# Three edits to the order of roundings in a fused attention and feed-forward kernel: ScalarE's rounding of g goes ahead of the next tanh, and the rounding of the softmax weights goes from ScalarE to VectorE

## The chip, the cores and the metric

The kernel runs on one core of one Trainium2 chip. The metric is the device time of one execution, in microseconds (us). Five queues matter: TensorE (PE in the profile; its weight loads are PEld), VectorE (DVE), ScalarE (ACT), GpSimd (POOL) and the DMA queue of SyncE (SP). Each works through its own instructions in order; an instruction waits at the head of its queue until what it reads is ready and what it writes is free.

## The reference

Four batches of 12480 rows, width 128, 49 agents. Attention goes through the agents, then a feed-forward layer of width 2048 with the activation h - tanh(h):

```python
a2k = softmax(scale * agents @ k^T)      # 49 x 12480 per batch
agent_v = a2k @ v                        # 49 x 128
q2a = softmax(scale * q @ agents^T)      # 12480 x 49
x = q2a @ agent_v                        # 12480 x 128
h = x @ w_in                             # 12480 x 2048
g = h - tanh(h)
out = g @ w_out                          # 12480 x 128
```

Everything is float32.

## The kernel before, in words

**Blocks, steps, pairs.** The rows are cut into 100 blocks of 500 (25 per batch). A block takes eight steps, each for two of the 16 chunks of the hidden width; so there are 800 steps. Two blocks are a pair of 16 steps, and `pos` (0 to 15) is the place of a step in its pair. The two matrices ahead of h are folded: `awh` and `awl` are the high and low part of `agent_v @ w_in` (98 rows: the 49 agents twice, for the high and low part of the weights), so that h comes from the softmax weights p in one product.

**One step.** For step k, in the names of the profile:

- `first_product` (`m1`, L537 and L538): four matmuls of 500 columns on TensorE make h(k) in PSUM, which has three buffers for h. It is issued two steps ahead.
- `tanhs` (`tanh`, L546): ScalarE makes y = tanh(c h). `squares` (`square`, L551): ScalarE makes z = y². Both are issued one step ahead.
- `product` (`mul`, L556): VectorE makes g = h z (for the small h of these inputs h - tanh(h) is a constant times that, to the accuracy needed). h comes from PSUM, z from SBUF.
- `high` (L589 on GpSimd, L587 on ScalarE): the high part gh of g, rounded to float32r, a format in which a matmul takes one pass. `low` (`low`, L594): VectorE makes gl = g - gh, one step later, behind the product of that step.
- `out` (`m2`, L606, L607, L609): six matmuls on TensorE, four that read gh and then two that read gl, are added in PSUM. It follows `low`, so TensorE's order is m1(k+2), m2(k-1), m1(k+3), m2(k).
- In every second block the last step (`PLAIN_PAIR`, pos 7 of a pair) is "plain": g isn't split at all; two chunks go through four-pass float32 matmuls (L603), and neither GpSimd's rounding nor VectorE's subtraction is made for it.

The rounding of g is GpSimd's in all steps but 39. Those 39 are the steps in which GpSimd has to subtract the row maximum of attention scores (`av`, L321): there `product` only leaves a mark (`ET.Activation`) in the list `r1`, and ScalarE makes gh one step later. They are at pos 1, 3 and 12 (`VS`) of those pairs in which the weighted sum over v of the next batch is made: 13 groups of keys for each of three batches.

**The side work.** For the next batch, `phase1` makes key scores (at pos 3, 5 and 14, `KS`, 13 pairs in all) and after that the sums over v (pos 1, 3, 12, another 13 pairs' worth). For the next pair of blocks, `q_softmax` makes the weights p from q: 64 small matmuls at pos 3, row maximum and copy at pos 4 with GpSimd's subtraction (L504), exp at pos 6, and at pos 8 the norm on VectorE: sum, add, reciprocal, multiply (L508 to L511). Its steps are parted by `yield`; `QGAPS` says how many steps lie between. At pos 9 ScalarE rounds p to its high part (L514), and at pos 10 GpSimd subtracts it from p (L516) for the low part. `q_transpose` (L524, L529) transposes both at pos 12 to 15. The first two of the 50 softmaxes are made before or early in the main loop with gaps of 1; 48 use `QGAPS`.

**What sets the order.** It is written out by hand: the loop in `fast` issues each step's parts in a fixed sequence, and `issue_order` chains the instructions of VectorE, ScalarE, GpSimd and TensorE in the order in which they were issued. In a step k the loop calls `tanhs(k + 1)`, then the copy of a finished block to its output (L770), then lets all side jobs advance by one `yield`, then `squares(k + 1)` (with the marked rounding of step k - 1 ahead of the square), `first_product(k + 2)`, `product(k)`, `low` for step k - 1, `out` for step k - 1.

Of the kernel before, what the change touches and what calls it, by code (L numbers as in the profile page):

```python
# [17 lines left out]
ET = mybir.EngineType  # L18
# [6 lines left out]
A = 49  # L25
# [6 lines left out]
TT = 126  # L32
# [31 lines left out]
AHEAD = 2  # L64
QL = 0
QS = 2
QGAPS = (1, 1, 0, 2, 2, 1, 1)
T0 = 12
T1 = 14
KS = (3, 5, 14)  # L70
# [4 lines left out]
def width(n):  # L75
    return min(BLK, N - n % NBLK * BLK)
# [22 lines left out]
class Build:  # L99
# [384 lines left out]
    def q_softmax(self, halves, qt, res, TT=TT, gaps=(1,) * 7):  # L484
        nc = self.nc
        yield from (None,) * gaps[0]
        ps = self.misc()
        for t in range(GT):
            b, at, w = halves[t // BT]
            at += min(t % BT * TT, w - TT)  # L490
            for r in range(0, TT, QUART):
                m = min(QUART, TT - r)
                to = ps[r : r + m, t * A : (t + 1) * A]
                nc.tensor.matmul(to, qt[:, at + r : at + r + m], self.ag[:, b, :], start=True, stop=True)  # L494
        yield from (None,) * gaps[1]
        pv = ps[:TT, : GT * A].rearrange("p (t a) -> p t a", a=A)
        m = self.small.tile([128, GT], F32, tag="qm", name="qm")
        e = self.small.tile([128, GT, A], F32, tag="qe", name="qe")
        ev = e[:TT]
        s = self.small.tile([128, GT], F32, tag="qs", name="qs")  # L500
        nc.vector.tensor_reduce(m[:TT], pv, axis=AX.X, op=ALU.max)
        nc.scalar.copy(ev, pv)  # L502
        yield from (None,) * gaps[2]
        nc.gpsimd.tensor_tensor(ev, ev, m[:TT, :, None].broadcast_to([TT, GT, A]), ALU.subtract)  # L504
        yield from (None,) * gaps[3]
        nc.scalar.activation(ev, ev, AF.Exp, scale=SCALE)
        yield from (None,) * gaps[4]
        nc.vector.tensor_reduce(s[:TT], ev, axis=AX.X, op=ALU.add)  # L508
        nc.vector.tensor_scalar(s[:TT], s[:TT], EPS, None, ALU.add)
        nc.vector.reciprocal(s[:TT], s[:TT])  # L510
        nc.vector.tensor_tensor(ev, ev, s[:TT, :, None].broadcast_to([TT, GT, A]), ALU.mult)  # L511
        yield from (None,) * gaps[5]
        pp = self.small.tile([128, GT, A2], F32R, tag="pp", name="pp")
        nc.scalar.copy(pp[:TT, :, :A], ev)  # L514
        yield from (None,) * gaps[6]
        nc.gpsimd.tensor_tensor(pp[:TT, :, A:], ev, pp[:TT, :, :A].bitcast(F32), ALU.subtract)  # L516
        res.append(pp)
# [132 lines left out]
    def fast(self):  # L650
        nc, tc = self.nc, self.tc
# [4 lines left out]
        qt, pp, pT = {}, {}, {}  # L656
# [5 lines left out]
        def q_job(p):  # L662
            pp[p] = []
            w = width(2 * p), width(2 * p + 1)
            halves = (blocks[2 * p][0], 0, w[0]), (blocks[2 * p + 1][0], w[0], w[1])
            return self.q_softmax(halves, qt.pop(p), pp[p], gaps=QGAPS if p > 1 else (1,) * 7)

# [4 lines left out]
        with ExitStack() as first:  # L672
# [34 lines left out]
            at = self.count() - 1  # L707
# [48 lines left out]
        r1, r2, done = [], [], []  # L756
# [21 lines left out]
                hs[k] = self.m1(self.aw[blocks[n][0]], pT[n][0], i, width(n))  # L778

        def tanhs(k):  # L780
            if k < len(steps):
                ys[k] = self.tanh(hs[k], width(steps[k][0]))

        def squares(k):
            for n, at in enumerate(r1):
                if at[3] is ET.Activation:
                    r1[n] = at[:3] + (self.high(at[2], True),)
            if k < len(steps):
                zs[k] = self.square(ys.pop(k))

# [22 lines left out]
        for k in range(AHEAD):  # L813
            first_product(k)
        tanhs(0)
        squares(0)
        for k, (n, i) in enumerate(steps):
            b = blocks[n][0]
            pos = (n % 2) * HP + i
            p = n // 2  # L820
            if n % NBLK == 0 and i == 0 and b + 1 < B:
                kq = self.phase1(b + 1)
            tanhs(k + 1)
            while done and done[0][1] < k - 1:
                finish(done.pop(0)[0])
# [9 lines left out]
            for gen in live:  # L835
                try:
# [3 lines left out]
                    pass  # L840
            live[:] = nxt
            squares(k + 1)
            first_product(k + AHEAD)
            begin = kq and n and pos in kq[0][0]
# [90 lines left out]
```

## Time and profile before

| what | value |
|---|---|
| median of 3 runs | 2160.22 us (2155.68 to 2160.96) |
| the profiled execution | 2158.05 us, span 2156.3 us |
| granted TensorE clock | 0.997 |
| VectorE busy | 1980.1 us of the span, 92% |
| ScalarE busy | 1814.4 us, 84% |
| GpSimd busy | 1387.0 us, 64% |
| rounding by ScalarE (L587) | 39 times, 1.037 us each |
| rounding of p by ScalarE (L514) | 50 times, 0.520 us each |

A row of the timeline is: start in us, duration in us, engine, line of the kernel, operation, tile written <- tiles read, shapes, count; in square brackets the idle time of the engine just before it and what ended it. A row of the waits is: engine and line that waited <- engine and line that released it: us in total, times, longest. A row of the windows is: stretch in us, its length, and the busy time and instructions of each engine. Matmul rows overlap, because matmuls are pipelined: the distance from start to start is what a matmul costs.

### The profile page before, as it was taken

What the parts mean: (1) busy time and instruction counts of PE and PEld (TensorE: products, weight loads), DVE (VectorE), ACT (ScalarE), POOL (GpSimd) and SP (SyncE); (2) the same over time, 40 slices, a digit from 0 to 9 for tenths busy, and PEclk for the clock granted to TensorE, in tenths of its full rate; (3) what the DMA queues carried; (4) which work ended last, traced back from release to release, by engine and by line L of the source; (5) the groups of instructions that cost most, each with busy time, mean ns of one, the idle gap of its engine ahead of it and who ended that gap; (6) DMA issues with size and microseconds to landing.
All of it is one profiled execution on the core that took longest, in us unless ns stands there. A gap on an engine that the chain in (4) does not pass through costs nothing.

```text
span 2156.3 us, 37634 instructions
## 1 busy us (share of the span) xinstructions
PE 2093.9 (97%) x14885; PEld 1633.4 (76%) x14885; DVE 1980.1 (92%) x2028; ACT 1814.4 (84%) x2136; POOL 1387.0 (64%) x857
## 2 busy tenths in 40 slices
PE   7999999999999999999999999999999999999998
PEld 7577777777777777777777777777777787877876
DVE  7899998889999998888999999888899999999998
ACT  3888888888888888888888888888888888988887
POOL 0466765556767665565676667656576777767776
PEclk9999999999999999999999999999999999999999
DMA  9222112110111121112002210121010010000000
GB/s 355 71 79 69 42 41 67 59 51 29 39 50 49 57 64 49 49 45 74 20 20 63 74 33 20 50 67 41 19 39 20 20 39 20 28 31 20 29 11 21
DMA packets 65352, 109.16 MB, mean 51 GB/s; under 512 B 3984, under 2 KB 44176, under 8 KB 65168
## 3 DMA queue, kind: packets, MB, share of 16 engines
q1 hardware_dynamic: 65168, 106.68, 15.1%
q8 instruction: 119, 1.95, 0.4%
q14 instruction: 65, 0.53, 0.1%
HBM read 81.10 MB, written 25.56 MB: 49 GB/s over the span
## 4 chain that ended last, share of the span: by engine, by line
PE 58%; DVE 22%; ACT 8%; issue 7%; POOL 4%; DMA 0%; POOLq 0%; SPq 0%; DVEq 0%; ACTq 0%
PE h L537 12%; PE misc L609 11%; DVE gl L594 11%; PE h L538 11%; PE misc L606 8%; PE misc L607 8%; DVE g L556 8%; POOL gh L589 3%; ACT z L551 2%; PE misc L336 2%; ACT gh L587 2%; PE misc L603 1%; ACT y L546 1%; PE misc L494 1%; PE h L249 1%
## 5 line engine op out<-in xcount | busy, mean ns | idle before, releaser
L589 POOL TENSOR_SCALAR gh<-g 128x1000 fp32r<-128x1000 f32 (+1 forms) x704 | 1214.0, 1724 | 600.2 <-DVE g L556 513.5
L546 ACT ACTIVATE y<-h 128x1000 f32<-128x1000 f32 (+1 forms) x800 | 805.9, 1007 | 270.5 <-PE h L538 267.0
L556 DVE TENSOR_TENSOR g<-h,z 128x1000 f32<-128x1000 f32 (+1 forms) x800 | 950.2, 1190 | 80.0 <-ACT z L551 74.4
L594 DVE TENSOR_TENSOR gl<-g,gh 128x1000 fp32r<-128x1000 f32 (+1 forms) x743 | 926.0, 1246 | 63.7 <-ACT gh L587 56.8
L551 ACT ACTIVATE z<-y 128x1000 f32<-128x1000 f32 (+1 forms) x800 | 834.4, 1043 | 14.5 <-DVE g L556 1.0
L537 PE MATMUL h<-pT,awh 98*128 98x500 f32 (+1 forms) x1600 | 669.8, 419 | 2.2 <-ACT awh L460 1.5
L538 PE MATMUL h<-pT,awl 98*128 98x500 f32 (+1 forms) x1600 | 622.3, 389 | 0.4 <-DVE awl L463 0.4
L606 PE MATMUL misc<-gh,wo_l 128*128 128x500 f32 (+1 forms) x1486 | 580.3, 390 | 13.1 <-ACT gh L587 12.6
L607 PE MATMUL misc<-gh,wo_h 128*128 128x500 f32 (+1 forms) x1486 | 575.4, 387 | 0.0
L609 PE MATMUL misc<-gl,wo_h 128*128 128x500 f32 (+1 forms) x1486 | 466.6, 395 | 28.1 <-DVE gl L594 25.7
L537 PEld LDWEIGHTS h<-pT,awh 98*128 98x128 f32 x1600 | 300.6, 188 | 84.9 <-issue 19.6
L609 PEld LDWEIGHTS misc<-gl,wo_h 128*128 128x128 f32 x1486 | 270.0, 188 | 116.4 <-DVE gl L594 68.3
L538 PEld LDWEIGHTS h<-pT,awl 98*128 98x128 f32 x1600 | 302.4, 189 | 66.5 <-issue 14.5
L606 PEld LDWEIGHTS misc<-gh,wo_l 128*128 128x128 f32 x1486 | 279.6, 188 | 85.7 <-ACT gh L587 29.1
L607 PEld LDWEIGHTS misc<-gh,wo_h 128*128 128x128 f32 x1486 | 280.7, 189 | 54.3
L504 POOL TENSOR_TENSOR qe<-qe,qm 126x392 f32<-126x392 f32 x50 | 52.5, 1050 | 111.4 <-ACT qe L502 111.4
L321 POOL TENSOR_TENSOR s<-s,mb 128x392 f32<-128x392 f32 (+1 forms) x39 | 70.2, 1801 | 41.3 <-DVE g L556 41.3
L603 PE MATMUL misc<-g,wo_f 128*128 128x500 f32 (+1 forms) x196 | 90.1, 581 | 0.0
L770 ACT ACTIVATE o<-misc 128x500 f32<-128x500 f32 (+1 forms) x100 | 58.2, 582 | 5.3 <-PE misc L609 5.3
L529 ACT CAST pT<-misc 98x500 fp32r<-98x500 f32 (+1 forms) x100 | 56.7, 568 | 1.8 <-PE misc L524 1.8
L603 PEld LDWEIGHTS misc<-g,wo_f 128*128 128x128 f32 x196 | 37.0, 189 | 26.3 <-issue 22.6
L516 POOL TENSOR_TENSOR pp<-qe,pp 126x392 fp32r<-126x392 f32 x50 | 49.3, 985 | 7.5 <-ACT pp L514 7.5
(104 smaller groups left out, 843.5 us busy)
## 6 DMA issues: line engine op xcount, KB each, us to landing
kt<-kT SPq DMA_DIRECT2D x48, 512.0 KB, 3.8
qt<-qT SPq DMA_DIRECT2D x46, 500.0 KB, 3.5
outT<-o SPq DMA_DIRECT2D x46, 500.0 KB, 2.6
v<-v SPq DMA_DIRECT2D x36, 512.0 KB, 4.0
vt<-v SPq DMA_DIRECT2D x12, 512.0 KB, 7.2
raw<-w_in SPq DMA_DIRECT2D x4, 512.0 KB, 9.2
v<-w_out SPq DMA_DIRECT2D x4, 512.0 KB, 8.7
qt<-qT SPq DMA_DIRECT2D x4, 490.0 KB, 3.3
```

The source lines that it names most:

```text
L321: (nc.gpsimd if b else nc.vector).tensor_tensor(e3, sv, top, ALU.subtract)
L537: nc.tensor.matmul(h[:, c, :w], aw[0][:A2, sl], pT[:A2, :w], start=True, stop=False)
L538: nc.tensor.matmul(h[:, c, :w], aw[1][:A2, sl], pT[:A2, :w], start=False, stop=True)
L546: self.nc.scalar.activation(self.pair(y), h, AF.Tanh, scale=TSC)
L551: self.nc.scalar.activation(z, y, AF.Square)
L556: self.nc.vector.tensor_tensor(self.pair(g), h, self.pair(z), ALU.mult)
L589: self.nc.gpsimd.tensor_scalar(gh, g, 1.0, 0.0, ALU.mult, ALU.add)
L594: self.nc.vector.tensor_tensor(gl, g, gh.bitcast(F32), ALU.subtract)
L603: nc.tensor.matmul(acc[:, :w], wf[:, c * C : (c + 1) * C], gh[:, x], start=f == 0, stop=f == NCH - 1)
L606: nc.tensor.matmul(acc[:, :w], self.wo_l[:, f, :], gh[:, x], start=f == 0, stop=False)
L607: nc.tensor.matmul(acc[:, :w], self.wo_h[:, f, :], gh[:, x], start=False, stop=False)
L609: nc.tensor.matmul(acc[:, :w], self.wo_h[:, f, :], gl[:, x], start=False, stop=f == NCH - 1)
```

## The change

Three places. In `q_softmax`, with the last two gaps of `QGAPS` now 0, VectorE instead of ScalarE makes the high part of p, right behind the multiply of the norm at pos 8, and GpSimd's subtraction of it is issued at once, in the same step and ahead of that step's rounding of g. That is the step behind the plain one, which has no `low` on VectorE. Softmaxes with a gap (the first two) keep ScalarE. And the loop over `r1` that issues ScalarE's marked roundings moves from `squares` to the head of `tanhs`: a rounding of g(k - 1) now stands ahead of tanh(k + 1), the output copy and the side jobs of step k, and no longer behind them.

```diff
-QGAPS = (1, 1, 0, 2, 2, 1, 1)
+QGAPS = (1, 1, 0, 2, 2, 0, 0)
...
         pp = self.small.tile([128, GT, A2], F32R, tag="pp", name="pp")
-        nc.scalar.copy(pp[:TT, :, :A], ev)
+        (nc.scalar.copy if gaps[5] else nc.vector.tensor_copy)(pp[:TT, :, :A], ev)
         yield from (None,) * gaps[6]
         nc.gpsimd.tensor_tensor(pp[:TT, :, A:], ev, pp[:TT, :, :A].bitcast(F32), ALU.subtract)
...
         def tanhs(k):
-            if k < len(steps):
-                ys[k] = self.tanh(hs[k], width(steps[k][0]))
-
-        def squares(k):
             for n, at in enumerate(r1):
                 if at[3] is ET.Activation:
                     r1[n] = at[:3] + (self.high(at[2], True),)
+            if k < len(steps):
+                ys[k] = self.tanh(hs[k], width(steps[k][0]))
+
+        def squares(k):
             if k < len(steps):
                 zs[k] = self.square(ys.pop(k))
```

More of the change, by code (lines that the diff above doesn't have):

```diff
@@ L780, in tanhs @@
         def tanhs(k):
+            for n, at in enumerate(r1):
+                if at[3] is ET.Activation:
+                    r1[n] = at[:3] + (self.high(at[2], True),)
             if k < len(steps):
@@ L784, in squares @@
         def squares(k):
-            for n, at in enumerate(r1):
-                if at[3] is ET.Activation:
-                    r1[n] = at[:3] + (self.high(at[2], True),)
             if k < len(steps):
```

## The prediction

> **What bounds the kernel now.** I read the page's busy shares first, then the windows over single pairs, then who waited for whom, then the timeline of each engine through one pair.
>
> ```profile
> PE 2093.9 (97%) x14885; PEld 1633.4 (76%) x14885; DVE 1980.1 (92%) x2028; ACT 1814.4 (84%) x2136; POOL 1387.0 (64%) x857
> ```
>
> ```profile
> 1762.82:1801.52 38.70, 38.55 (x232) 30.87 (x231) 37.44 (x36) 34.56 (x40) 28.58 (x18) 1.00 0.08 28
> 875.23:920.76 45.53, 43.57 (x280) 32.81 (x279) 38.94 (x39) 38.48 (x46) 26.59 (x18) 1.00 0.19 58
> ```
>
> Each window is one pair of blocks (pos 0 to 15). The first has no side work for the next batch: TensorE is busy 38.55 of 38.70 us and sets the time, with VectorE close behind at 37.44. The second is a pair with the three ScalarE roundings. It takes 45.53 us, but TensorE is busy only 43.57, VectorE 38.94 and ScalarE 38.48: no engine is full, so something waits.
>
> ```profile
> DVE gl L594 <- ACT gh L587: 56.8, 39, 1.7
> ...
> PE misc L609 <- DVE gl L594: 25.7, 57, 1.1
> ```
>
> VectorE waits for ScalarE's rounding at each of the 39, 1.46 us on average, and TensorE waits for gl in turn. Since TensorE is the bound, I count its lost time, from the starts of its matmuls.
>
> ```profile
> 882.25 0.40 PE L538 MATMUL h<-pT,awl 98*128 98x500 f32 x1
> 882.87 0.49 PE L606 MATMUL misc<-gh,wo_l 128*128 128x500 f32 x1 [0.22 <-ACT gh L587]
> ...
> 883.65 0.39 PE L607 MATMUL misc<-gh,wo_h 128*128 128x500 f32 x1
> 884.10 0.71 PE L609 MATMUL misc<-gl,wo_h 128*128 128x500 f32 x2
> ...
> 887.50 0.62 PE L609 MATMUL misc<-gl,wo_h 128*128 128x500 f32 x2
> ...
> 888.65 0.39 PE L538 MATMUL h<-pT,awl 98*128 98x500 f32 x1
> 889.56 0.50 PE L606 MATMUL misc<-gh,wo_l 128*128 128x500 f32 x1 [0.52 <-ACT gh L587]
> ...
> 890.36 0.38 PE L607 MATMUL misc<-gh,wo_h 128*128 128x500 f32 x1
> 891.61 0.73 PE L609 MATMUL misc<-gl,wo_h 128*128 128x500 f32 x2 [0.87 <-DVE gl L594]
> ```
>
> From 882.87 to 883.65 lie three starts; the first of them is 0.10 long over the usual 0.39, so the usual distance is (0.78 - 0.10) / 3 = 0.23. At pos 1 TensorE loses 882.87 - 882.25 - 0.23 = 0.39 waiting for gh, 0.10 on the slow restart, 0.22 waiting for gl, and 0.09 on that restart (0.71 against the undisturbed 0.62 of 887.50): 0.80 us. At pos 3, worked out in the same way from the last four rows, it loses 0.68 + 0.11 + 1.02 + 0.11 = 1.92 us.
>
> **The change, part one: the rounding ahead of tanh.** Nothing is added or removed; on ScalarE one instruction of 1.03 us is passed by the tanh, the output copy, and the exp and copy of the side jobs. TensorE, GpSimd, VectorE and SP keep their order. These are VectorE and then ScalarE in the same pair, with g(2), gl(1), g(3), g(4), gl(3), and the gl of pos 12:
>
> ```profile
> 880.26 1.20 DVE L556 TENSOR_TENSOR g<-h,z 128x1000 f32<-128x1000 f32 x1 [0.31 <-ACT z L551]
> 882.85 1.20 DVE L594 TENSOR_TENSOR gl<-g,gh 128x1000 fp32r<-128x1000 f32 x1 [1.39 <-ACT gh L587]
> 883.96 1.19 DVE L556 TENSOR_TENSOR g<-h,z 128x1000 f32<-128x1000 f32 x1
> ...
> 886.66 1.19 DVE L556 TENSOR_TENSOR g<-h,z 128x1000 f32<-128x1000 f32 x1
> 889.54 2.02 DVE L594 TENSOR_TENSOR gl<-g,gh 128x1000 fp32r<-128x1000 f32 x1 [1.69 <-ACT gh L587]
> ...
> 914.67 1.20 DVE L594 TENSOR_TENSOR gl<-g,gh 128x1000 fp32r<-128x1000 f32 x1 [1.37 <-ACT gh L587]
> ```
>
> ```profile
> 879.18 1.04 ACT L551 ACTIVATE z<-y 128x1000 f32<-128x1000 f32 x1
> 880.41 1.01 ACT L546 ACTIVATE y<-h 128x1000 f32<-128x1000 f32 x1 [0.19 <-PE h L538]
> ...
> 881.78 1.03 ACT L587 CAST gh<-g 128x1000 fp32r<-128x1000 f32 x1
> ...
> 884.67 1.04 ACT L551 ACTIVATE z<-y 128x1000 f32<-128x1000 f32 x1
> 886.78 1.01 ACT L546 ACTIVATE y<-h 128x1000 f32<-128x1000 f32 x1 [1.07 <-PE h L538]
> ...
> 888.47 1.04 ACT L587 CAST gh<-g 128x1000 fp32r<-128x1000 f32 x1
> 889.40 1.06 ACT L551 ACTIVATE z<-y 128x1000 f32<-128x1000 f32 x1
> ```
>
> ```profile
> 878.93 1.84 POOL L321 TENSOR_TENSOR s<-s,mb 128x392 f32<-128x392 f32 x1 [0.50 <-DVE g L556]
> ...
> 889.47 1.05 POOL L589 TENSOR_SCALAR gh<-g 128x1000 fp32r<-128x1000 f32 x1
> ```
>
> Pos 1, worked through: GpSimd's subtraction, which waits for g(1), starts at 878.93, so g(1) is there long before ScalarE is free. An instruction on ScalarE follows another by 0.93 (888.47 to 889.40). Behind the square of 879.18 the rounding starts at 880.11 and ends at 881.14, instead of 882.81. The tanh moves from 880.41 to 881.04; the square follows it by what the rounding did before (881.78 - 880.41 = 1.37), at 882.41, and ends at 883.46. VectorE's gl(1) follows g(2) by 1.11 (882.85 to 883.96): 881.37, no wait. g(3) then waits for z until 883.49, against 883.96: 0.47 earlier. TensorE's first L606 finds gh at 882.48, and L609 at 883.38 finds gl(1), ended at 882.57. All 0.80 goes. The later tanh costs nothing because z is still earlier than the old g(3); with z 0.5 later it would begin to cost.
>
> Pos 3: g(3) ends at 884.68. The square of 884.67 moves forward by 0.3 (its tanh follows the square of 882.41 by 0.93, and it the tanh by 1.03), to 884.37; the rounding follows at 885.30 and ends at 886.34. The tanh started on its h at 886.78; h is 0.80 earlier, 885.98, so tanh follows the rounding at 886.23: the rounding goes into what was idle time (1.07). Its square comes 1.69 behind (888.47 - 886.78), at 887.92, ending 888.98 and not 890.46. gl(3) stands behind g(4) (886.66 - 0.47 = 886.19), at 887.30, and ends at 888.49. TensorE reaches m2(3) at 888.65 - 0.80 + 0.23 = 888.08 and its L609 at 888.98: both waits go, 1.92 us. Also gone is the length of that gl: 2.02 us instead of 1.20, because GpSimd's rounding started 0.07 ahead of it at 889.47.
>
> What is late next: GpSimd subtracts the row maximum (L504) right before that rounding; it can't run beside gl(3) and so ends about 889.4, the rounding of g(4) about 890.45. gl(4), which VectorE could start at 889.0 + 1.11 = 890.1, starts at 890.5 and ends at 891.7. TensorE has m2(3), the sixteen matmuls over v and the next m1 ahead of m2(4), and wants that gl at about 892.4. 0.7 us of cover.
>
> Pos 12 has the wait of pos 1 (1.37 against 1.39), one copy between tanh and rounding as there: again 0.80. Sum: 13 x (0.80 + 1.92 + 0.80) = 46 us. Bounds: at worst the part that hangs on GpSimd comes back (below); more than 46 can't come from here, as TensorE then has no wait left at these places.
>
> **Part two: p's high part on VectorE.** It removes a ScalarE copy at pos 9 and a GpSimd subtraction at pos 10, and puts a VectorE copy and that subtraction into pos 8, ahead of g(8) and of GpSimd's rounding of it. One pair with key scores, pos 8 to 11, beside VectorE's one cast of the trace:
>
> ```profile
> L127 DVE CAST identr<-ident x1: 227/227/227, 1.3 to 1.3; 128x128 fp32r<-128x128 f32 x1
> ```
>
> ```profile
> 728.07 1.19 DVE L556 TENSOR_TENSOR g<-h,z 128x1000 f32<-128x1000 f32 x1
> ...
> 729.44 1.03 POOL L589 TENSOR_SCALAR gh<-g 128x1000 fp32r<-128x1000 f32 x1 [5.54 <-DVE g L556]
> ...
> 729.65 1.20 DVE L556 TENSOR_TENSOR g<-h,z 128x1000 f32<-128x1000 f32 x1 [0.39 <-ACT z L551]
> ...
> 730.76 1.19 DVE L594 TENSOR_TENSOR gl<-g,gh 128x1000 fp32r<-128x1000 f32 x1
> ...
> 732.15 0.61 PE L609 MATMUL misc<-gl,wo_h 128*128 128x500 f32 x2
> ...
> 732.82 0.96 POOL L516 TENSOR_TENSOR pp<-qe,pp 126x392 fp32r<-126x392 f32 x1
> ...
> 733.00 1.83 DVE L594 TENSOR_TENSOR gl<-g,gh 128x1000 fp32r<-128x1000 f32 x1
> ...
> 734.19 0.39 PE L607 MATMUL misc<-gh,wo_h 128*128 128x500 f32 x1
> ...
> 734.89 0.72 PE L609 MATMUL misc<-gl,wo_h 128*128 128x500 f32 x2 [0.31 <-DVE gl L594]
> ```
>
> The new copy has 392 elements. Below, it is bounded by the 128-element cast, 0.23 us; above by three times that, 0.68. I take 0.38, since a fixed part must be in the 0.23, so it grows less than the size does. g(8) goes from 728.07 to about 728.48, its end to 729.68. The subtraction (0.96) fits on GpSimd, idle 5.54 us there, before gh(8), which moves from 729.44 to 729.83 and ends at 730.86. g(9) waits for z anyway (0.39): the shift is hidden. gl(8) starts at 730.90 and ends at 732.09: TensorE wants it at 732.15. At pos 10 gl(9) is no longer stretched (1.83 against 1.19, because L516 stands ahead of it by 0.18); it ends near 734.3, and TensorE's loss of 0.70 - 0.23 + 0.11 = 0.58 goes. ScalarE is relieved of a copy.
>
> I take 0.58 in the 13 pairs with key scores (7.5 us). In the 13 with roundings I take nothing: TensorE has side work there that covers it. In the other 22 VectorE is fuller (first window), g(9) waits less, and gl(8) comes up to 0.4 late: between 0 and 0.58, I take 0.2 (4.4). Together 12 us. With 0.23 for the copy, gl(8) is in time nearly everywhere: 7.5 + 22 x 0.48 = 18. With 0.68 it is 0.3 late in the 13 pairs, which with a slow restart leaves 0.2 of 0.58 (2 us), and costs the other 22 up to 0.3 each (7): -5.
>
> **Sum.** 2158.05 (span 2156.3 and 1.75 around it; 2.2 below the median of the runs) - 46 - 12 = 2100 us.
>
> **The rivals.** (a) *GpSimd takes the place of ScalarE at pos 4*: if L504 or the rounding behind it takes 0.7 longer than I think, gl(4) decides and the second half of the loss at pos 3 comes back: 13 x 1.13 = 15 us, 2115. For it: GpSimd's L321 takes 1.84 us beside gl. Against: the 0.7 of cover. (b) *GpSimd's subtraction holds g(8)* as it holds gl(9): g(8) then waits for 0.15 + 0.96 more, gl(8) misses TensorE by 1.1 in 48 pairs, 53 us on top of the forecast: 2153. Against: the g of 880.26 runs its usual 1.20 us though L321 is at work until 880.77; what differs from gl is that g reads h from PSUM. The Trainium skill (SBUF — State Buffer, section "SBUF: two separate sides") calls the port pair that VectorE and GpSimd share an exclusive lock, held for a whole instruction, and names on VectorE's side the instructions in a two-port mode or with two inputs in SBUF. By that rule (b) can't come from g, but the new copy, if it runs in such a mode, could hold up GpSimd; the trace agrees on the lock in the 1.83 of gl(9), and shows GpSimd idle for 5.54 us where the copy goes, so the rule lowers the chance of (b) and leaves the sum. (c) *Slower: the rounding blocks ScalarE.* It now waits for g(k-1) at the head of the queue with tanh, copies and square behind it. If g(k-1) ends later than ScalarE gets free, tanh and z go back by that, g(k+1) with them, and h is held longer, so the loop feeds its own delay. The margin is 1.2 us at pos 1 and 0.6 at pos 3 (884.68 to 885.30). From a negative margin on it costs up to 0.93 a time, 39 times, 36 us with no gain: 2194 without part two. Against: rounding and square were both ahead of g(k+1) before too. (d) *No effect*: the waits are those of another semaphore than named, and the order moves nothing: 2158.
>
> **How the numbers follow.** Forecast 0.68, (a) 0.15, (b) 0.07, (d) 0.05, (c) 0.05. The range takes the forecast with its bounds (18 for part two: 2094, and a little for the runs' spread: 2090) and (a) with almost nothing left of part two (2115 + 11 = 2126). Faster by over 0.3% (6.5 us, about what a measurement of this kernel tells from none) has the forecast, (a) and half of (b): 0.87; same (d) and the rest of (b): 0.08; slower (c): 0.05.
>
> **What would show it.** Right: the wait of gl for ACT gh gone from the list; the pair with roundings at about 42 us; all gl near 1.2 us at pos 4 and 10; a VectorE cast of 0.38; no TensorE wait for gl at pos 10. Wrong: a new wait of gl for POOL gh at pos 5 or of L609 at pos 9, g(8) over 1.3 us, a rounding that waits on g.

## The result, and the profile after

The changed kernel takes 2104.78 us in the median of four runs (2102.5 to 2104.99), the one before, in the same series, 2157.95 (2154.74 to 2160.96). The ratio is 0.9751, with a 95% interval of 0.9733 to 0.977. The profiled execution went from 2158.05 to 2104.99 us, 53 us less; 58 were forecast.

First the page of the changed kernel, engines' busy time, and its windows over three pairs: without side work, with ScalarE's roundings, with key scores. The columns are those of the windows of before.

```profile
PE 2072.6 (99%) x14885; PEld 1642.1 (78%) x14885; DVE 1958.9 (93%) x2076; ACT 1796.8 (85%) x2088; POOL 1409.8 (67%) x857
```

```profile
1711.40:1749.90 38.50, 38.50 (x232) 30.89 (x231) 37.14 (x37) 34.39 (x39) 28.50 (x18) 1.00 0.08 27
852.90:894.86 41.96, 41.96 (x280) 33.30 (x279) 38.01 (x41) 37.84 (x45) 28.53 (x18) 1.00 0.21 63
687.32:728.95 41.63, 41.54 (x424) 32.90 (x423) 38.75 (x41) 34.96 (x42) 28.25 (x18) 1.00 0.21 64
```

The pair with roundings fell from 45.53 to 41.96 us, and TensorE is busy through all of it. The pair without side work fell from 38.70 to 38.50. Twelve pairs hold three roundings each, at pos 1, 3 and 12, and three more pairs hold one, at pos 12. At 3.57 us for the twelve and 0.8 for the three, roundings account for 45 of the 53 us.

The waits of the changed kernel no longer hold VectorE's gl behind ScalarE's gh (56.8 us before), nor TensorE's L606 behind it. TensorE's remaining wait for gl, seen at the weight load, is less than half:

```profile
PEld misc L609 <- DVE gl L594: 29.8, 47, 1.6
```

Before it was 68.3 us, 97 times. Now ScalarE, VectorE and TensorE through pos 1 to 5 of the pair whose rows were shown of before (it starts at 852.90 and started at 875.23):

```profile
857.79 1.02 ACT L587 CAST gh<-g 128x1000 fp32r<-128x1000 f32 x1
858.71 0.99 ACT L546 ACTIVATE y<-h 128x1000 f32<-128x1000 f32 x1
859.61 0.58 ACT L770 ACTIVATE o<-misc 128x500 f32<-128x500 f32 x1
860.07 1.04 ACT L551 ACTIVATE z<-y 128x1000 f32<-128x1000 f32 x1
...
862.98 1.01 ACT L587 CAST gh<-g 128x1000 fp32r<-128x1000 f32 x1
863.89 1.00 ACT L546 ACTIVATE y<-h 128x1000 f32<-128x1000 f32 x1
```

```profile
857.92 1.20 DVE L556 TENSOR_TENSOR g<-h,z 128x1000 f32<-128x1000 f32 x1 [0.30 <-ACT z L551]
859.04 1.19 DVE L594 TENSOR_TENSOR gl<-g,gh 128x1000 fp32r<-128x1000 f32 x1
861.14 1.20 DVE L556 TENSOR_TENSOR g<-h,z 128x1000 f32<-128x1000 f32 x1 [0.91 <-ACT z L551]
...
863.84 1.19 DVE L556 TENSOR_TENSOR g<-h,z 128x1000 f32<-128x1000 f32 x1
864.95 1.19 DVE L594 TENSOR_TENSOR gl<-g,gh 128x1000 fp32r<-128x1000 f32 x1
866.66 1.20 DVE L556 TENSOR_TENSOR g<-h,z 128x1000 f32<-128x1000 f32 x1 [0.53 <-ACT z L551]
867.88 1.20 DVE L594 TENSOR_TENSOR gl<-g,gh 128x1000 fp32r<-128x1000 f32 x1
```

```profile
859.92 0.40 PE L538 MATMUL h<-pT,awl 98*128 98x500 f32 x1
860.15 0.39 PE L606 MATMUL misc<-gh,wo_l 128*128 128x500 f32 x1
```

The rounding has no idle time ahead of it in either place, gl follows g without a wait, no gl here is over 1.2 us, and TensorE goes from m1 to m2 in 0.23 us where it had taken 0.62. VectorE now waits for z instead (0.91 and 0.53): that is idle time of an engine that isn't the bound. Over the whole trace, 63 gl took more than 1.3 us before; after, four did, all in the first 105 us.

Last, pos 8 to 10 of a pair with key scores, VectorE, ScalarE, GpSimd and TensorE of the changed kernel:

```profile
710.45 0.37 DVE L514 CAST pp<-qe 126x392 fp32r<-126x392 f32 x1
710.73 0.56 DVE L279 TENSOR_REDUCE s<-misc 128x49 f32<-128x392 f32 x1
711.21 1.19 DVE L556 TENSOR_TENSOR g<-h,z 128x1000 f32<-128x1000 f32 x1
712.78 1.20 DVE L556 TENSOR_TENSOR g<-h,z 128x1000 f32<-128x1000 f32 x1 [0.39 <-ACT z L551]
713.89 1.19 DVE L594 TENSOR_TENSOR gl<-g,gh 128x1000 fp32r<-128x1000 f32 x1
...
716.11 1.19 DVE L594 TENSOR_TENSOR gl<-g,gh 128x1000 fp32r<-128x1000 f32 x1
```

```profile
711.32 0.49 ACT L285 COPY s<-misc 128x392 f32<-128x392 f32 x1 [0.96 <-DVE s L279]
711.71 1.04 ACT L551 ACTIVATE z<-y 128x1000 f32<-128x1000 f32 x1
```

```profile
712.58 1.03 POOL L589 TENSOR_SCALAR gh<-g 128x1000 fp32r<-128x1000 f32 x1 [0.72 <-DVE g L556]
```

```profile
714.66 0.39 PE L607 MATMUL misc<-gh,wo_h 128*128 128x500 f32 x1
715.14 0.72 PE L609 MATMUL misc<-gl,wo_h 128*128 128x500 f32 x2
```

gl(9) is 1.19 us long (1.83 before), as forecast. But TensorE now loses time one step earlier, at pos 9's matmuls for gl(8): 715.14 - 714.66 - 0.23 = 0.25 and 0.1 on the restart, where nothing was forecast. GpSimd's rounding of g(8) ended at 713.61, before gl(8) started; gl(8) follows g(9) by the usual 1.11, so it is late because g(9) is. (The expectations below count the matmuls for gl(8) to pos 10 and those for gl(9) to pos 11.)

### The profile page after: what moved, and what is told of

It is laid out like the page before. It is cut to its first block, busy times and chain, and to the rows that moved or that the text cites. A ratio compares the mean times of both kernels' runs of the same rounds, so it can differ in the third digit from the quotient of the medians.

```text
span 2102.9 us, 37664 instructions
## 1 busy us (share of the span) xinstructions
PE 2072.6 (99%) x14885; PEld 1642.1 (78%) x14885; DVE 1958.9 (93%) x2076; ACT 1796.8 (85%) x2088; POOL 1409.8 (67%) x857
## 4 chain that ended last, share of the span: by engine, by line
PE 83%; DVE 11%; ACT 3%; issue 2%; POOL 1%; DMA 0%; POOLq 0%; SPq 0%; DVEq 0%; ACTq 0%
PE h L537 16%; PE h L538 15%; PE misc L609 15%; PE misc L606 14%; PE misc L607 14%; DVE g L556 4%; DVE gl L594 3%; PE misc L603 2%; PE misc L336 2%; PE misc L494 2%; PE h L249 1%; PE misc L524 1%; PE misc L277 1%; ACT z L551 1%; ACT y L546 1%
## 5 line engine op out<-in xcount | busy, mean ns | idle before, releaser
L589 POOL TENSOR_SCALAR gh<-g 128x1000 fp32r<-128x1000 f32 (+1 forms) x704 | 1230.8, 1748 | 347.0 <-DVE g L556 337.0
L594 DVE TENSOR_TENSOR gl<-g,gh 128x1000 fp32r<-128x1000 f32 (+1 forms) x743 | 887.3, 1194 | 7.5 <-POOL gh L589 1.8
L606 PE MATMUL misc<-gh,wo_l 128*128 128x500 f32 (+1 forms) x1486 | 576.6, 388 | 0.5 <-POOL gh L589 0.5
L609 PE MATMUL misc<-gl,wo_h 128*128 128x500 f32 (+1 forms) x1486 | 461.1, 391 | 10.8 <-DVE gl L594 9.5
L538 PEld LDWEIGHTS h<-pT,awl 98*128 98x128 f32 x1600 | 302.2, 189 | 65.8 <-issue 13.6
L609 PEld LDWEIGHTS misc<-gl,wo_h 128*128 128x128 f32 x1486 | 274.0, 188 | 81.4 <-DVE gl L594 29.8
L606 PEld LDWEIGHTS misc<-gh,wo_l 128*128 128x128 f32 x1486 | 279.7, 188 | 59.7 <-POOL gh L589 3.3
```

What stands on the lines that cost most here:

```text
L538: nc.tensor.matmul(h[:, c, :w], aw[1][:A2, sl], pT[:A2, :w], start=False, stop=True)
L589: self.nc.gpsimd.tensor_scalar(gh, g, 1.0, 0.0, ALU.mult, ALU.add)
L594: self.nc.vector.tensor_tensor(gl, g, gh.bitcast(F32), ALU.subtract)
L606: nc.tensor.matmul(acc[:, :w], self.wo_l[:, f, :], gh[:, x], start=f == 0, stop=False)
L609: nc.tensor.matmul(acc[:, :w], self.wo_h[:, f, :], gl[:, x], start=False, stop=f == NCH - 1)
```

## The experiments

Two theories stood against each other at first. Mine: TensorE is the bound, its waits are local, and each part takes away its own. The rival: the parts, or the places, depend on each other, because a delay at one step can be made good by slack at the next.

**Only the rounding ahead of tanh.**

```diff
-QGAPS = (1, 1, 0, 2, 2, 0, 0)
+QGAPS = (1, 1, 0, 2, 2, 1, 1)
```

> ScalarE's rounding ahead of tanh, softmax weights as before. Theory: TensorE is the bound and each part takes away its own waits, so the parts add up: 13 x 3.52 = 46 us come from here, 2158 - 46 = 2112 us; the pair with roundings takes about 41.9 us, and TensorE still loses 0.5 to 0.6 us at pos 11 of the other pairs, as before. Rival: the two parts need each other (a loss that is taken away at pos 1 to 4 is made good again at pos 10 and 11 by the old softmax order): then about 2125 us or more.

Measured: 2111.39 us against 2159.89 of before (ratio 0.9773, 0.9757 to 0.9789). The windows over a pair with roundings and one with key scores:

```profile
855.28:897.23 41.95, 41.95 (x280) 33.29 (x279) 38.22 (x40) 38.09 (x46) 28.51 (x18) 1.00 0.21 63
689.01:730.84 41.83, 41.53 (x424) 32.84 (x423) 39.05 (x39) 35.23 (x43) 28.22 (x18) 1.00 0.20 64
```

Within 0.02 us the first has the 41.96 of the full change, the second the 41.85 of before. The theory stands.

**Only the softmax weights.** The kernel before with the new `QGAPS` and VectorE's copy; the loop over `r1` stays in `squares`.

> Only the softmax weights' high part on VectorE and the low part at once; rounding of g behind tanh as before. Theory: 13 pairs with key scores give 0.25 each and 22 others 0.2 each, as in the changed kernel, none in the pairs with roundings: 2158 - 7.5 = about 2150 us. Rival by the prediction's own sizes: 12 us, 2146. Rival: the gain needs the first part: 2158.

Measured: 2150.66 (0.9953, 0.9937 to 0.997). The windows in the other order, key scores and then roundings:

```profile
705.82:747.47 41.65, 41.56 (x424) 32.91 (x423) 38.76 (x41) 34.95 (x42) 28.24 (x18) 1.00 0.20 64
875.86:921.39 45.53, 43.55 (x280) 32.82 (x279) 38.74 (x40) 38.18 (x45) 26.56 (x18) 1.00 0.19 58
```

0.20 in a pair with key scores, nothing in one with roundings (45.53 as before). The median alone, with an interval of 6.5 to 13.6 us for the gain, doesn't exclude the 12 us of the first rival; the 0.20 in the window speaks against it. Within their intervals the two parts add up: 48.5 and 9.2 us below the kernel before, against 53 to 55 for both.

**Early only at pos 3.**

```diff
+EARLY_AT = (3,)
...
+        def marked(places):
             for n, at in enumerate(r1):
-                if at[3] is ET.Activation:
+                if at[3] is ET.Activation and (at[0] % 2) * HP + at[1] in places:
                     r1[n] = at[:3] + (self.high(at[2], True),)
...
         def tanhs(k):
+            marked(EARLY_AT)
...
         def squares(k):
+            marked(VS)
```

> The changed kernel, but the roundings of pos 1 and pos 12 stand behind tanh again; only that of pos 3 is early. Theory: the losses are local, 0.80 us each at pos 1 and pos 12, 13 times: 2105 + 21 = 2126 us, and VectorE's gl waits for ScalarE 26 times. Rival: a delay at one place is made good by slack at the next: under 2115 us.

Measured: 2125.38 (0.9841, 0.9824 to 0.9857), and VectorE waits for ScalarE's rounding 27 times. The added lines move the kernel's line numbers by one:

```profile
DVE gl L595 <- ACT gh L588: 37.9, 27, 1.5
```

The places are 27 and not 26: 12 at pos 1 and 15 at pos 12. 20.6 us come back, 0.76 each, where 0.80 was read from TensorE's starts; the lengths of the pairs in the two traces give 0.82. The losses are local.

**VectorE rounds at pos 8, GpSimd subtracts at pos 10.**

```diff
-QGAPS = (1, 1, 0, 2, 2, 0, 0)
+QGAPS = (1, 1, 0, 2, 2, 0, 2)
```

> The changed kernel, but GpSimd makes the low part of the softmax weights at pos 10 as before; the high part stays on VectorE at pos 8. Theory (the gain of part two is that GpSimd's subtraction no longer stands ahead of gl(9)): gl(9) is stretched to 1.8 us again, 0.5 us in 13 + 22 pairs, and the cost of the copy on VectorE stays: about 2120 us, above the 2112 of the kernel with the first part alone. Rival (the gain is that ScalarE is relieved of a copy): stays at 2105.

Measured: 2126.84 (0.9846, 0.983 to 0.9863), 15 us above the kernel with the first part alone. Pos 10, VectorE and GpSimd:

```profile
1752.76 1.85 DVE L594 TENSOR_TENSOR gl<-g,gh 128x1000 fp32r<-128x1000 f32 x1
```

```profile
1752.60 0.95 POOL L516 TENSOR_TENSOR pp<-qe,pp 126x392 fp32r<-126x392 f32 x1
```

The stretch is back: gl starts 0.16 behind GpSimd's subtraction and takes 1.85 us. So relieving ScalarE is not what pays. VectorE's copy alone is a loss; the gain is where GpSimd's subtraction lies. The size was missed by 7 us: by the traces a pair without roundings takes 0.6 us longer than in the changed kernel, where 0.5 was put down, and one with roundings 0.26, where nothing was. In the pair shown, the late gl(8) of pos 9 and the stretched gl(9) of pos 10 each cost TensorE a restart too (L609 takes 0.73 and 0.72 us there, undisturbed 0.62).

**ScalarE rounds at pos 9, GpSimd subtracts at once.**

```diff
-QGAPS = (1, 1, 0, 2, 2, 0, 0)
+QGAPS = (1, 1, 0, 2, 2, 1, 0)
```

> The changed kernel, but ScalarE makes the high part of the softmax weights at pos 9 as before, and GpSimd subtracts in the same step, ahead of its rounding of g(9). Theory (the subtraction must run where VectorE reads one input from PSUM): it now falls on gl(8), both wait for each other, the rounding of g(9) is late instead: no gain over the first part alone, 2112. Rival (one step earlier is enough, whichever engine rounds): 2105.

Measured: 2129.27 (0.9868, 0.9853 to 0.9883), worse than either said. VectorE and GpSimd at pos 9 of a pair with key scores:

```profile
722.29 1.19 DVE L594 TENSOR_TENSOR gl<-g,gh 128x1000 fp32r<-128x1000 f32 x1
```

```profile
722.53 1.78 POOL L516 TENSOR_TENSOR pp<-qe,pp 126x392 fp32r<-126x392 f32 x1 [0.54 <-ACT pp L514]
```

```profile
725.33 2.01 DVE L594 TENSOR_TENSOR gl<-g,gh 128x1000 fp32r<-128x1000 f32 x1 [0.72 <-POOL gh L589]
```

GpSimd waits 0.54 for ScalarE, then for gl(8), and its rounding of g(9) stands behind all that, so that gl(9) waits 0.72 for it and then takes 2.01 us. One step earlier is not enough with ScalarE's rounding. This run doesn't part the wait for ScalarE from the meeting with gl(8); what it shows is that the subtraction came too late, and VectorE's copy buys an earlier start for it, beside a g. The loss isn't in every pair: the six pairs in which VectorE also folds the next batch's matrix (L463, L471) take 0.4 us less than in the changed kernel. As I read it, that is because VectorE has no copy to make there at pos 8; no run shows it by itself.

**The copy twice.**

```diff
         (nc.scalar.copy if gaps[5] else nc.vector.tensor_copy)(pp[:TT, :, :A], ev)
+        if not gaps[5]:
+            nc.vector.tensor_copy(pp[:TT, :, :A], ev)
```

> The changed kernel with VectorE's copy of the softmax weights made twice, the same values to the same place. Theory (at pos 8 VectorE's time is on the path in the 35 pairs without roundings, and covered in the 13 with them): 0.33 to 0.37 more each, 2105 + 12 = 2117 us. Rival (the copy is covered by the four-pass matmuls of the plain step): 2105 to 2107.

Measured: 2117.29 (0.981, 0.9795 to 0.9825). A pair with key scores, then one with roundings:

```profile
691.20:733.27 42.07, 41.78 (x424) 32.84 (x423) 39.12 (x41) 34.93 (x42) 28.20 (x18) 1.00 0.20 63
858.16:900.16 42.00, 42.00 (x280) 33.25 (x279) 38.29 (x42) 37.82 (x45) 28.42 (x18) 1.00 0.20 63
```

0.44 more in the first, 0.04 in the second: at pos 8 VectorE is on the path, except in the pairs with the sums over v. That TensorE's work on these sums is what covers the copy is my reading; no run takes that work away.

**Key scores first at pos 8.** This tests the step that failed (below).

```diff
-            for gen in live:
+            for gen in reversed(live) if pos == 8 else live:
...
-            live[:] = nxt
+            live[:] = reversed(nxt) if pos == 8 else nxt
```

> The changed kernel, but at pos 8 the side jobs advance in the reverse order: VectorE's row maximum of the key scores (L279) comes ahead of the norm and the copy. Theory (the gain of part two in the 13 pairs with key scores fell short because the copy delays L279, L279 the copy L285 on ScalarE, that the square, z and g(9)): ScalarE's square is 0.37 earlier there, TensorE's loss of 0.32 at pos 10 goes, 13 times: 2105 - 4 = 2101 us. Rival (it fell short because GpSimd's subtraction delays the rounding of g(8)): the loss stays, 2105.

Measured: 2100.19 (0.9735, 0.972 to 0.975). ScalarE at pos 8, and the window over that pair:

```profile
706.64 0.48 ACT L285 COPY s<-misc 128x392 f32<-128x392 f32 x1
707.01 1.05 ACT L551 ACTIVATE z<-y 128x1000 f32<-128x1000 f32 x1
```

```profile
683.71:725.09 41.38, 41.38 (x424) 32.89 (x423) 38.76 (x40) 35.06 (x42) 28.43 (x18) 1.00 0.20 64
```

The copy of the scores on ScalarE no longer waits, and the pair goes from 41.63 to 41.38; over the 13 pairs the traces give 2.7 us, and nothing in the others. The theory stands. The medians differ by 4.6 us, but of that 2.3 lies, by the traces, in the first pair of blocks and ahead of it, where other kernels with the same order there (that with only pos 3 early is one) vary as much. By the ratios to the kernel before, 0.9735 and 0.9751 with intervals that overlap, the step from the changed kernel to this one couldn't be told; the pairs show it.

**The norm behind g(8).**

```diff
             for gen in live:
+                if gen is late and pos == 8:
+                    continue
...
             product(k, values)
+            if late is not None and pos == 8:
+                run(late)
+                late = None
             low(1)
```

> The changed kernel, but at pos 8 the norm, the copy and GpSimd's subtraction are issued behind the product of that step: g(8) and GpSimd's rounding of it come first. Theory (what is left of the loss at pos 10 comes from g(8) standing behind 1.9 us of norm and copy): gh(8) is ready 1.5 us earlier, gl(8) follows g(9) at once, 0.3 us less in 35 pairs and more in the six pairs that lose 1.0 there: about 2092 us. Rival: GpSimd's subtraction now falls on gl(8) and stretches it, as it did with gl(9) before: 2110 or more.

Measured: 2115.89 (0.9805, 0.9792 to 0.9818). My theory fell. But the rival's mechanism wasn't it either: GpSimd's subtraction ran beside a g, and gl kept its 1.19. GpSimd and VectorE at pos 8:

```profile
1738.91 1.03 POOL L589 TENSOR_SCALAR gh<-g 128x1000 fp32r<-128x1000 f32 x1 [2.59 <-DVE g L556]
```

```profile
1739.26 0.71 DVE L509 TENSOR_SCALAR qs<-qs 126x8 f32<-126x8 f32 x1
```

An addition on eight numbers a row takes 0.71 us instead of 0.17, and ends just behind GpSimd's rounding (1739.97 and 1739.94; in all 48 of these softmaxes it ends 0.02 to 0.03 behind). Now that g(8) comes first, GpSimd rounds it while VectorE does the norm.

**Without that addition.** For softmax sums of 1 and more, adding 1e-9 changes nothing in float32; both kernels leave it out in the queries' softmax. The first has the norm behind g(8), the second the key scores first.

```diff
-        nc.vector.tensor_scalar(s[:TT], s[:TT], EPS, None, ALU.add)
```

> The kernel with the norm behind g(8), without the addition of 1e-9. There the addition took 0.71 us and not 0.17, while GpSimd rounded g(8). Theory (VectorE's instruction was held by GpSimd's lock on the shared port pair, and the next that takes the pair is held in its place): the multiply L511, with two inputs in SBUF, or the reciprocal ahead of it ends only after GpSimd's rounding; 0.2 to 0.3 gained in 35 pairs: 2106 to 2109 us. Rival (the addition is slow behind a reduce for another reason): reciprocal 0.20 and multiply 0.57 as ever, 0.7 gained: 2093 or less.

> The kernel with scores first at pos 8, and without the addition of 1e-9 to the softmax sums (L509 of the queries' softmax; the sum is 1 or more, so in float32 the addition changes nothing). Theory (what is left of TensorE's loss at pos 10 is g(8) behind the norm and copy on VectorE): g(8) and all behind it is 0.21 earlier, the 0.1 to 0.2 and the slow restart of 0.1 go in 35 pairs: 2100 - 7 = 2093 us. Rival (z or GpSimd decides there): 2100.

Measured, norm behind g(8): 2098.26 (0.9722, 0.9707 to 0.9737); GpSimd and then VectorE at pos 8, where L509 and L510 are now the reciprocal and the multiply:

```profile
1726.20 1.03 POOL L588 TENSOR_SCALAR gh<-g 128x1000 fp32r<-128x1000 f32 x1 [2.59 <-DVE g L555]
```

```profile
1726.54 0.20 DVE L509 RECIPROCAL qs<-qs 126x8 f32<-126x8 f32 x1
1726.78 0.86 DVE L510 TENSOR_TENSOR qe<-qe,qs 126x392 f32<-126x392 f32 x1
```

The reciprocal runs unhindered beside GpSimd's rounding, the multiply takes 0.86 instead of 0.57 and ends 0.41 after it, in all 48. So the wait passed to the next instruction with two inputs in SBUF, as the theory said. The gain was more than I had put down, since the addition itself goes as well: 0.54 + 0.17 saved, 0.29 lost, 0.42 in 35 pairs, 15 of the 18 us by which the medians differ.

Measured, key scores first: 2094.86 (0.9704, 0.9691 to 0.9717). g(8) is 0.2 earlier and that reaches the end, as expected. This is the lowest median of the study.

**The maximum of the folded matrix one step later**, on top of the last one.

```diff
             if bound and b:
+                yield
                 self.bound(b, c, sl)
```

> The kernel without the addition of 1e-9, and VectorE's maximum of the folded matrix (L471) made one step later. It stands between g(8) and g(9) in the six pairs in which TensorE loses 1.0 at pos 10. Theory (gl(8) is late there because VectorE has both): 0.6 less in six to eight pairs: 2093 - 4 = 2089 us. Rival (VectorE is full in those pairs and the loss moves to the next step): 2093.

Measured: 2095.53 (0.9711, 0.9698 to 0.9724), no different. The window over such a pair and TensorE's waits for gl(8) and gl(9) in it, first without and then with the delay (two kernels):

```profile
1546.18:1586.84 40.66, 40.04 (x236) 31.46 (x235) 39.34 (x40) 34.97 (x41) 28.18 (x18) 1.00 0.07 26
...
1573.17 0.72 PE L608 MATMUL misc<-gl,wo_h 128*128 128x500 f32 x2 [0.62 <-DVE gl L593]
```

```profile
1545.73:1586.74 41.01, 40.38 (x236) 31.38 (x235) 39.42 (x40) 34.99 (x41) 28.21 (x18) 1.00 0.07 26
...
1572.47 0.72 PE L609 MATMUL misc<-gl,wo_h 128*128 128x500 f32 x2 [0.36 <-DVE gl L594]
...
1575.27 0.72 PE L609 MATMUL misc<-gl,wo_h 128*128 128x500 f32 x2 [0.27 <-DVE gl L594]
```

The rival was right: VectorE is busy 39.3 of 40.7 us there, and moving one of its instructions only moves the wait. TensorE's one wait of 0.62 became two of 0.36 and 0.27, and the pair got 0.35 longer.

## Why the prediction was right, and by how much it was off

**The bound.** That TensorE sets the time held where it was counted: the pair with roundings got shorter by what TensorE had lost in it, 3.57 for a forecast 3.52 us. The same 3.57 us rule out rival (d), no effect.

**Part one, 46 us.** Confirmed by the kernel that has it alone (48.5 below the kernel before, in an interval of 46 to 52) and step by step. g(3) was to start 3.23 behind g(2): 861.14 - 857.92 = 3.22. g(5) was to start 2.83 behind g(4): 866.66 - 863.84 = 2.82. gl(4) was to wait for GpSimd until 1.5 behind g(5); it came 1.22 behind, so rival (a) had even less room than I gave it. One term was miscounted: the 39 roundings are not 13 at each place but 12 at pos 1, 12 at pos 3 and 15 at pos 12, which makes the sum 44.6 instead of 46 us. That is too little to show in the result.

**Rival (b)**, GpSimd's subtraction holding g(8): g(8) runs 1.19 us (711.21). **Rival (c)**, ScalarE blocked by the rounding: there was no idle time ahead of the rounding in any of the 39.

**Part two, 12 us: mis-sized.** The copy took 0.365 (0.38 taken), gl(9) lost its stretch, and the other 22 pairs gave the 0.2 each that I took (38.70 to 38.50 in the one shown). That 0.2 was a pick between 0 and 0.58 and not worked out, so its hit is luck. In the 13 pairs with key scores I forecast 0.58 and got 0.22 (41.85 to 41.63): 4.7 of the 5 us by which the sum missed the profile. The difference of 0.36 a pair is what TensorE lost at pos 9 (0.25 and the restart), a wait of L609 that I had named as a sign of being wrong. The step that failed is the sentence "g(9) waits for z anyway (0.39): the shift is hidden". The wait was real, but z hung on the same VectorE. These rows of the kernel before, VectorE and ScalarE, are from the pair that I had worked through:

```profile
727.60 0.56 DVE L279 TENSOR_REDUCE s<-misc 128x49 f32<-128x392 f32 x1
```

```profile
728.19 0.49 ACT L285 COPY s<-misc 128x392 f32<-128x392 f32 x1 [0.57 <-DVE s L279]
```

ScalarE's copy of the key scores waits for VectorE's maximum, and the square for z stands behind that copy. The new copy on VectorE goes ahead of L279, so z moves back with it: ScalarE's wait grew from 0.57 to 0.96, VectorE's wait for z stayed 0.39. I had taken as slack a wait that the change itself feeds. Putting L279 first gave about 3 us of the 4.7 back.

## What to carry to other kernels

Count lost time on the engine that is the bound, from start to start of its instructions and place by place; here that gave 0.80 and 1.92 us a place. The runs came within a few hundredths for the three places of a pair together (3.57 for 3.52) and at 0.76 to 0.82 for the 0.80. Before a wait is used as cover for a moved instruction, follow what is waited for back to its own source: if it leads to the engine that gets the new work, there is no cover. And what an instruction costs can depend on what another engine does at the same time (0.17 or 0.71 us for one addition here), so look for a place beside an instruction that doesn't get in its way.

## What the runs showed of the hardware

- An addition over 126x8 numbers took 0.71 us instead of 0.17 beside GpSimd's rounding; a multiply with two SBUF inputs 0.86 instead of 0.57; the reciprocal beside the same rounding its usual 0.20, and g, with h from PSUM, its usual 1.19 beside GpSimd's subtraction of p. The Trainium skill (SBUF — State Buffer, section "Who interferes with whom") lists copies, casts and `tensor_scalar` among VectorE's instructions that can take the shared pair, and says that two inputs in SBUF contend as well, with a GpSimd instruction that reads SBUF; these runs agree for the addition (a `tensor_scalar`) and for two inputs, down to an instruction of eight columns.
- A matmul of 500 columns on TensorE that has waited for gh or gl is followed by the next after 0.33 instead of 0.23 us: such a wait costs 0.1 on top of itself. In the kernel before this holds for all 127 that started more than 0.12 us late.
